# Bfloat16 constants loaded into place, first weights requested ahead of them, row statistics moved behind the queries: the opening of a four-layer attention kernel

## The chip, the cores and the metric

The kernel runs on one core of a Trainium2 chip. The metric is the device time of one execution in microseconds (us). Three runs of the kernel before the change took 3129.34, 3132.39 and 3118.13 us; their median is 3129.34.

Engines are named as in the profile: PE is the matrix engine, DVE the vector engine, ACT the scalar engine, POOL GpSimd. SP issues DMAs and computes nothing; POOL issues DMAs too. Each engine works through its own instructions strictly in the order in which they stand.

## The reference, cut to what matters

Two layers alternate twice on x, a float32 array of 2048 rows (tokens) by 512 columns.

```
x = x + A(layernorm(x));  x = x + B(layernorm(x));  and both once more
A: q = x@wq in 32 heads of 16; one shared k = x@wk and v = x@wv (16 wide)
   softmax(q k / 4) v for every head, then @ wo
B: 32 heads, 4 segments of 512 tokens; causal attention within a segment,
   joined by the gate sigmoid(beta) with a running memory of earlier segments, then @ wo
layernorm: (x - mean) / sqrt(var + 1e-5), no weights
```

## The kernel before

Tokens go in four blocks (b = 0 to 3) of 512, and a block in four tiles of 128 rows. Numbers that need more than bfloat16 are kept as a high and a low part (`xh`, `xl` for the normed and transposed input, `w[:, 0]` and `w[:, 1]` for a weight), so a projection of one block is 12 matmuls of 512 columns: high by high, high by low, low by high, for each of four slices of 128 input columns. All four tiles of a block must be in `xh` and `xl` before its projection can start.

The program is generated by coroutines. `prep()` makes layer A's keys for block after block: `norm_tiles` (normalise on DVE into `xn`, transpose on PE, copy to `xh`, subtract to `xl`), `a_keys` (project K, split it into float16 parts, write `kst` and `va`), and for block 0 `a_queries`. `norm_stats` computes mean and variance of a block's rows: BN_STATS and BN_AGGR for each tile, then some twelve tiny operations for the inverse root. While block b is at work, `prep()` loads the x tiles of block b+1 and issues their `norm_stats` ahead of time; the `xt` pool has four buffers, so each load waits until a tile of block b has been normalised.

Each of the four queries projections of block 0 takes its weight from `wload`: POOL requests the float32 weight into a `wst` buffer, POOL writes the high part, DVE subtracts to make the low part (line 306), and POOL stores both parts to memory for later use. There are two `wst` buffers. Before the change they also hold, one after another, the constant masks on the way to their bfloat16 copies, and `w0`, the K and V weight. Query parts are written to memory by SP (`sd`, line 656) and read back in the layout of the scores (`qa`, lines 699 and 700).

A score tile is eight small matmuls (`qa`, `kst`), two heads by 512 queries for 128 keys; ACT takes its exponential into `pa` (line 790); two score tiles are followed on PE by eight matmuls with `va`, which accumulate in the banks `pva`. When a unit (a pair of head groups over a range of keys) ends, DVE transposes `pva` away (lines 828 and 829), and only then can the next unit's products start. The first 64 score tiles of the kernel need the keys of block 0 alone: eight units of four key tiles. Then come units of twelve key tiles, whose first eight need blocks 1 and 2 and the last four block 3. So the 81st score tile is the first that needs block 3.

`weave` mixes the score coroutine with `prep()` by a planner's clock: every generator step says when, by fixed costs, it will be ready, and the one with the best estimate is recorded next. The recorded steps are then placed by the tile framework's scheduler. An edit of the beginning can therefore move instructions well beyond it.

Of the kernel before, what the change touches and what calls it, by code (L numbers as in the profile page):

```python
# [29 lines left out]
F32 = mybir.dt.float32  # L30
F32R = mybir.dt.float32r
BF16 = mybir.dt.bfloat16
# [6 lines left out]
P = 128  # L39
S, D, H, DH = 2048, 512, 32, 16  # L40
NB, BT = 4, 512
# [10 lines left out]
TA0 = 60e3  # L52
TA1 = 110e3

C_ID, C_BM, C_SEL, C_MQ, C_MK, C_BN, C_BK, C_MV = 0, 128, 136, 144, 656, 784, 912, 1040
S_X, S_H, S_L, S_G = 0, 4, 5, 6
C_MW = C_MV + 512
C_N = C_MW + 512
# [2 lines left out]
def shape_constants():  # L61
    import numpy as np

    c = np.zeros((P, C_N), np.float32)
    r = np.arange(P)
    c[:, C_ID:C_ID + P] = np.eye(P)
    c[:, C_MQ + 384:C_MQ + 512] = np.where(r[None, :] > r[:, None], NEG, 0.0)
    c[:, C_MK:C_MK + P] = np.where(r[None, :] < r[:, None], NEG, 0.0)
    for t in range(4):
        for h in range(8):  # L70
            c[16 * h:16 * h + 16, C_BN + 32 * t + 8 * t + h] = 0.515625
    c[0:16, C_BK:C_BK + P] = 0.515625
    for t in range(4):
        for i in range(2):
            at = 32 * t + np.arange(32)
            c[64 * i:64 * i + 32, C_MV + P * t:C_MV + P * t + P] = np.where(r[None, :] < at[:, None], NEG, 0.0)
            c[64 * i:64 * i + 32, C_MW + P * t:C_MW + P * t + P] = np.where(r[None, :] > at[:, None], NEG, 0.0)
    for h in range(8):
        c[16 * h:16 * h + 16, C_BM + h] = 1.0
    for g, part in enumerate((0, 1, 0, 2, 1, 0)):  # L80
        c[16 * g:16 * g + 16, C_SEL + part] = 1.0
    c[96:98, C_SEL + 3] = -1.0
    for i in range(2):
        c[64 * i:64 * i + 16, C_SEL + S_H] = 1.0
        c[64 * i + 16:64 * i + 32, C_SEL + S_L] = 1.0
        c[64 * i + 32:64 * i + 48, C_SEL + S_H] = 1.0
        c[64 * i + 48, C_SEL + S_G] = -GUARD_K
    return c


@with_exitstack
def net_kernel(ctx, tc, x_in, a_wq, a_wk, a_wv, a_wo, b_wq, b_wk, b_wv, b_wo, b_beta, cst, out):
# [76 lines left out]
    def st(shape, dt, tag):  # L169
        return one.tile(shape, dt, tag=tag, name=nm(tag))  # L170

    def tmp(n, shape, dt, tag):
        return pools[n].tile(shape, dt, tag=tag, name=nm(tag))

    def f(ap):
        return ap.bitcast(F32)
# [36 lines left out]
        return r  # L213

    x_0 = load_x(0)
    cs = st([P, C_MQ], F32, "cs")
    nc.sync.dma_start(cs, cst[:, 0:C_MQ])
    c1 = tmp(2, [P, 512], F32, "wst")
    nc.sync.dma_start(c1, cst[:, C_MQ:C_MK])
    c2 = tmp(2, [P, 512], F32, "wst")[:, 0:C_MV - C_MK]  # L220
    nc.sync.dma_start(c2, cst[:, C_MK:C_MV])
    ident = cs[:, C_ID:C_ID + P]
    maskq = st([P, 512], BF16, "maskq")
    V.tensor_copy(maskq, c1)
    bmask = cs[:, C_BM:C_BM + 8]
    sel = [cs[:, C_SEL + i:C_SEL + i + 1] for i in range(7)]
    idb = st([P, P], BF16, "idb")
    V.tensor_copy(idb, ident)
    maskk = st([P, P], BF16, "maskk")
    V.tensor_copy(maskk, c2[:, C_MK - C_MK:C_MK - C_MK + P])  # L230
    bnq = st([P, 4, 32], BF16, "bnq")
    V.tensor_copy(bnq.rearrange("p t h -> p (t h)"), c2[:, C_BN - C_MK:C_BN - C_MK + P])
    bnk = st([P, P], BF16, "bnk")
    V.tensor_copy(bnk, c2[:, C_BK - C_MK:C_BK - C_MK + P])
    maskv = st([P, 4, P], BF16, "maskv")
    maskw = st([P, 4, P], BF16, "maskw")
    for m_, at in ((maskv, C_MV), (maskw, C_MW)):
        c3 = tmp(2, [P, 512], F32, "wst")
        nc.sync.dma_start(c3, cst[:, at:at + 512])
        V.tensor_copy(m_.rearrange("p c k -> p (c k)"), c3)  # L240
    ones = st([P, 32], BF16, "ones")
    G.memset(ones, 1.0)
    wmx = st([32, 8], F32, "wmx")
# [86 lines left out]


    wkv_d = dram.tile([P, 2, 512], F32, tag="wkv_d", name="wkv_d")
    w0 = tmp(2, [P, 512], F32, "wst")
    for r in range(8):
        src = (a_wv if r == 7 else a_wk).rearrange("(k p) c -> p k c", p=P)
        nc.sync.dma_start(w0.rearrange("p (k r c) -> p k r c", k=4, r=8)[:, :, r, :], src,
                          allow_slow_non_contiguous=True)
    w1 = tmp(6, [P, 2, 512], F32R, "w")
    V.tensor_copy(w1[:, 0, :], w0)  # L339
    V.tensor_tensor(w1[:, 1, :], w0, f(w1[:, 0, :]), op=ALU.subtract)  # L340
    nc.sync.dma_start(wkv_d, f(w1))
    wq_["ready"].append(("Akv", 0, w1))


# [165 lines left out]
    def norm_stats(xt, tiles, t0):  # L510

        n = len(tiles)
        mv = tmp(2, [P, 4, 2], F32, "mv")
        for j in range(n):
            s6 = tmp(2, [P, 6], F32, "s6")
            V.bn_stats(s6, xt[tiles[j]])
            V.bn_aggr(mv[:, j, :], s6)
        ve = tmp(2, [P, 4], F32, "ve")[:, 0:n]
        V.tensor_scalar_add(ve, mv[:, 0:n, 1], 1e-5)
        sh = tmp(2, [P, 4], I32, "sh")[:, 0:n]  # L520
        V.tensor_scalar(sh, ve.bitcast(I32), 1, None, op0=ALU.logical_shift_right)
        yi = tmp(2, [P, 4], I32, "yi")[:, 0:n]
        V.tensor_scalar(yi, sh, -1, 0x5F3759DF, op0=ALU.mult, op1=ALU.add)
        y = yi.bitcast(F32)
        for _ in range(3):
            y2 = tmp(2, [P, 4], F32, "y2")[:, 0:n]
            V.scalar_tensor_tensor(y2, y, -0.5, y, op0=ALU.mult, op1=ALU.mult)
            V.tensor_tensor(y2, y2, ve, op=ALU.mult)
            yn = tmp(4, [P, 4], F32, "yn")[:, 0:n]
            V.scalar_tensor_tensor(yn, y2, 1.5, y, op0=ALU.add, op1=ALU.mult)  # L530
            y = yn
        return mv, y, on("dve", t0, n * 700 + 2300)
# [88 lines left out]
    def a_queries(L, b, aw, early=False, spare=False):  # L621

        sqs = []

        def guard(a, z, tq):

            h = 8 * (z - a)
            ps, rel = yield from slot(lambda s: s[0:h, :], tq, "cols")
            for t in range(a, z):
                T.matmul(ps, lhsT=bnq[:, t, 8 * a:8 * z], rhs=sqs[t], start=t == a, stop=t == z - 1)  # L630
            mr = tmp(1, [32, 512], F16, "mr")[0:h]
            V.tensor_scalar_mul(mr, ps, UP * UP / GUARD_K)
            c = b if h == 32 else NB + a
            V.reduce_max(L["qmx"][0:h, c:c + 1], ps, axis=AX.X)  # L634
            nc.sync.dma_start(L["sd"][b][8 * a:8 * z, 32, :], mr)
            t1 = on("dve", pe(220 * (z - a), "cols"), 1200)
            rel(t1)
            return t1 + LOAD

        for t in range(4):  # L640
            w = aw[1 + t] if aw is not None else wget("Aq", 1)[0]
            ps, e, rel = yield from project_t(w)
            qf, t1 = evac(ps, e)
            rel(t1)
            if not L["exact"]:
                sq = tmp(4, [P, 512], BF16, "sqq")
                if spare:
                    V.tensor_tensor(sq, qf, qf, op=ALU.mult)
                    tq = on("dve", t1, 602)
                else:  # L650
                    A.activation(sq, qf, AF.Square)
                    tq = on("act", t1, 478)
                sqs.append(sq)
            qp, t1 = (split3 if L["exact"] else split2)(qf, t1)
            for c in range(3 if L["exact"] else 2):
                nc.sync.dma_start(L["sd"][b][8 * t:8 * t + 8, 16 * c:16 * c + 16, :], qp[:, c, :])
            t2 = t1 + LOAD
            if early:
                t2 = max(t2, (yield from guard(t, t + 1, tq)))
                L["qr"][b][t] = t2  # L660
        if not early:
            if not L["exact"]:
                t2 = max(t2, (yield from guard(0, 4, tq)))
            L["qr"][b] = [t2] * 4
# [556 lines left out]
    def everything(exact):  # L1221
# [21 lines left out]
        def prep():  # L1243
            for b in range(NB):
                if exact:
                    xt, st_ = load_x(b), None
                elif b == 0:
                    xt, st_ = x_0, None
                else:
                    xt, st_ = ahead.pop(b)  # L1250
                for tiles in ((0, 1), (2, 3)) if st_ is None else ((0, 1, 2, 3),):
                    yield from norm_tiles(xt, tiles, clk["pe"] + LOAD, st_)
                if b < NB - 1 and not exact:
                    xt = load_x(b + 1)
                    ahead[b + 1] = xt, norm_stats(xt, (0, 1, 2, 3), clk["pe"] + LOAD)
                yield from a_keys(L, b, aw)
                if b == 0 or exact:
                    yield from a_queries(L, b, aw, not exact)
                evac_on[0] = "dve"

        def late():
# [115 lines left out]
```

## Time and profile before

| | |
|---|---|
| runs | 3129.34, 3132.39, 3118.13 us |
| profiled execution | 3124.81 us, span 3123.0 us |
| granted PE clock, mean | 0.976 |
| PE busy | 2776.1 us (89%) |
| ACT busy | 2323.0 us (74%) |
| DVE busy | 1581.4 us (51%) |
| first score matmul / first query projection / K projection of block 0 start | 46.28 / 26.97 / 21.03 us |

The span runs from the first to the last instruction; the execution's time is 1.81 us more. Busy shares are means over the kernel. In the list of groups a row reads: line, engine, operation, output<-input with shapes, count, then busy time, mean length of one, and the idle time just before them with what ended it. In the timeline a row is start, length, engine, line, operation; a bracket gives the idle time before it and what ended it.

### The profile page before, as it was taken

How to read it: one execution, taken by the hardware profiler on the slowest of the kernel's cores; microseconds unless marked ns; L12 is line 12 of the kernel's file. 1: busy time of each engine (PE TensorE's matmuls, PEld its weight loads, DVE VectorE, ACT ScalarE, POOL GpSimd, SP SyncE). 2: the span in 40 equal slices, each digit the busy share in tenths (PEclk: the TensorE clock that was granted, in tenths of full speed). 3: DMA queues.
4: the chain of work that ended last, by engine and by line, in shares of the span. 5: the costliest groups of instructions: out<-in, count | busy, mean ns of one | idle time of the engine just before them, and what ended most of it. 6: DMA issues, size and time to landing. Idle time of an engine off the chain costs nothing.

```text
span 3123.0 us, 115586 instructions
## 1 busy us (share of the span) xinstructions
PE 2776.1 (89%) x51746; PEld 1324.5 (42%) x51746; DVE 1581.4 (51%) x4515; ACT 2323.0 (74%) x2519; POOL 278.4 (9%) x437
## 2 busy tenths in 40 slices
PE   6899888999898998889998898988998899898977
PEld 3444443445443453344544344434443445343543
DVE  6644345534555435564455545456345643555465
ACT  4788777886788767787688878668688887888433
POOL 2001120001000010000100010000000001000111
PEclk9999999999999999999999999999999999999978
DMA  5212231113311233112422142311331113211331
GB/s 156 79 53 81 91 121 47 40 61 108 102 40 42 68 106 95 39 43 71 136 78 73 38 137 96 122 48 51 115 97 45 42 30 127 66 42 46 127 106 38
DMA packets 153596, 242.30 MB, mean 78 GB/s; under 512 B 26272, under 2 KB 101888, under 8 KB 153088
## 3 DMA queue, kind: packets, MB, share of 16 engines
q1 hardware_dynamic: 124672, 132.03, 14.2%
q0 software_dynamic: 28416, 102.77, 10.3%
q8 instruction: 407, 6.67, 0.9%
q14 instruction: 101, 0.83, 0.1%
HBM read 164.21 MB, written 70.52 MB: 75 GB/s over the span
## 4 chain that ended last, share of the span: by engine, by line
PE 38%; ACT 24%; issue 18%; DVE 10%; DMA 6%; POOL 2%; SPq 1%; DVEq 0%; ACTq 0%; POOLq 0%
ACT pa L790 20%; PE bank L101 18%; PE bank L481 13%; PE bank L104 7%; ACT pa L1066 3%; DVE mo L1030 3%; DMA sb<-parts 3%; DMA xt<-in_A_x_dram 1%; DVE parts L579 1%; DMA qkb<-sb 1%; POOL parts L577 1%; DMA wst<-in_B_wk_dram 0%; PE bank L541 0%; DVE qf L559 0%; DVE m L1001 0%
## 5 line engine op out<-in xcount | busy, mean ns | idle before, releaser
L790 ACT ACTIVATE pa<-bank 128x1024 f32<-128x1024 f32 x2048 | 1952.1, 1041 | 458.2 <-PE bank L104 451.9
L104 PE MATMUL bank<-pa,va 64*17 64x512 f32 x14336 | 1101.9, 598 | 0.0
L101 PE MATMUL bank<-pa,va 64*17 64x512 f32 x2048 | 1057.7, 597 | 8.6 <-DVE ts L828 8.0
L101 PE MATMUL bank<-qa,kst 49*32 49x512 f16 x2048 | 741.5, 381 | 159.2 <-ACT pa L790 108.2
L104 PE MATMUL bank<-qa,kst 49*32 49x512 f16 x14336 | 816.8, 386 | 1.9 <-DVE qmx L634 1.9
L1030 DVE CUSTOM_DVE_ANT_0 mo<-bank,maskq 128x256 bf16<-128x256 f32 (+3 forms) x896 | 438.6, 490 | 297.6 <-PE bank L104 239.8
L104 PEld LDWEIGHTS <-kst 49*32 49x32 f16 x14336 | 224.3, 90 | 502.5 <-issue 490.9
L101 PE MATMUL bank<-qkb 48*32 48x384 f16 (+6 forms) x1472 | 331.3, 305 | 94.7 <-DVE m L1030 33.7
L1066 ACT ACTIVATE pa<-bank 128x1024 f32<-128x1024 f32 x320 | 317.4, 1033 | 82.9 <-PE bank L104 79.7
L104 PE MATMUL bank<-qkb 48*32 48x512 f16 (+7 forms) x6720 | 354.1, 311 | 12.4 <-DVE m L1001 10.8
L101 PEld LDWEIGHTS <-kst 49*32 49x32 f16 x2048 | 172.3, 91 | 382.6 <-issue 354.3
L481 PE MATMUL bank<-xh,w 128*128 128x512 f32 x832 | 296.9, 416 | 9.7 <-DVE w L339 4.5
L104 PEld LDWEIGHTS bank<-pa,va 64*17 64x17 f32 x14336 | 256.7, 94 | 26.1 <-DVE t L829 12.1
L481 PE MATMUL bank<-w,xh 128*128 128x512 f32 x752 | 244.6, 407 | 3.7 <-issue 2.0
L101 PEld LDWEIGHTS bank<-pa,va 64*17 64x17 f32 x2048 | 187.7, 94 | 105.4 <-issue 16.7
L104 PEld LDWEIGHTS <-qkb 50*32 50x32 f16 (+1 forms) x6720 | 151.1, 93 | 186.2 <-issue 177.7
L293 POOL DMA_DIRECT2D w<-wd x154 | 85.4, 554 | 1390.8 <-PE bank L481 1207.9
L481 PEld LDWEIGHTS bank<-xh,w 128*128 128x128 f32 x832 | 158.9, 191 | 85.3 <-issue 41.8
L101 PEld LDWEIGHTS <-qkb 48*32 48x32 f16 (+1 forms) x1472 | 123.5, 93 | 130.2 <-issue 86.3
L559 DVE COPY qf<-bank 128x512 f32<-128x512 f32 x91 | 62.8, 690 | 213.9 <-PE bank L481 213.9
L104 PE MATMUL bank<-pa,vb 128*17 128x384 f32 (+3 forms) x1920 | 165.3, 447 | 4.0 <-ACT pa L1066 3.6
L481 PE MATMUL bank<-xl,w 128*128 128x512 f32 x416 | 167.6, 403 | 0.2 <-DVE xl L549 0.2
(171 smaller groups left out, 2679.3 us busy)
## 6 DMA issues: line engine op xcount, KB each, us to landing
w<-wd POOLq DMA_DIRECT2D x154, 512.0 KB, 5.0
sb<-parts SPq DMA_DIRECT2D x192, 128.0 KB
qkb<-sb SPq DMA_DIRECT2D x256, 96.0 KB
wd<-w POOLq DMA_DIRECT2D x24, 512.0 KB, 4.0
x<-xt SPq DMA_DIRECT2D x48, 256.0 KB
xt<-x SPq DMA_DIRECT2D x48, 256.0 KB
qa<-sd SPq DMA_DIRECT2D x176, 66.0 KB
xt<-in_A_x_dram SPq DMA_DIRECT2D x40, 256.0 KB
```

Of the source, the lines that this page charges most:

```text
L101: nc.tensor.matmul(*a, **k)
L104: tc.keep_in_program_order(nc.tensor.matmul(*a, **k))
L293: G.dma_start(f(w), parts_d[kind, i])
L481: T.matmul(ps, lhsT=l_(kt), rhs=r_(kt), start=n == 0, stop=n == 11)
L559: V.tensor_copy(x, ps)
L577: G.tensor_scalar(parts[:, 0, :], x, up, 0.0, op0=ALU.mult, op1=ALU.add)
L579: V.scalar_tensor_tensor(parts[:, 1, :], x, up, parts[:, 0, :], op0=ALU.mult, op1=ALU.subtract)
L790: A.activation(x, sc, AF.Exp, scale=scale)
L1030: V.tensor_tensor_reduce(out=mo[:, 0:nk], in0=ps[:, o_:o_ + nk], in1=maskq[:, 512 - nk:512], op0=ALU.add, op1=ALU.max, scale=1.0, scalar=- ...
L1066: A.activation(e, sc, AF.Exp, scale=0.25 if exact else 0.25 / (UPB * UPB))
```

## The change

Four things, all in the opening of the program.

1. The masks and small matrices are stored in the constant array as bfloat16 pairs (rounded on the host) and are loaded straight into two tiles, `halves` (128x256 and 128x768 words, read as bfloat16). Seven DVE casts (`maskq`, `idb`, `maskk`, `bnq`, `bnk`, `maskv`, `maskw`) and the loads through `wst` are gone.
2. `w0` is requested right after the small constants and ahead of the larger masks and of the eight loads of the gate (`gv`); the same rows are fetched by four loads of 128x7x16 and one of 128x4x16 in place of eight of 128x4x16.
3. The store of the split K weight (`wkv_d`) is issued in `prep()` after the x tiles of block 1.
4. `norm_stats` of block b+1 is issued after `a_keys` (and `a_queries`) of block b; the load of its tiles stays where it was.

```diff
-C_ID, C_BM, C_SEL, C_MQ, C_MK, C_BN, C_BK, C_MV = 0, 128, 136, 144, 656, 784, 912, 1040
+C_ID, C_BM, C_SEL, C_HALF = 0, 128, 136, 144
+C_IB, C_MK, C_BN, C_BK, C_MQ, C_MV = 144, 272, 400, 528, 656, 1168
...
-    return c
+    c[:, C_IB:C_IB + P] = np.eye(P)
+    u = np.ascontiguousarray(c[:, C_HALF:]).view(np.uint32)
+    u = ((u + 0x7fff + ((u >> 16) & 1)) >> 16).astype(np.uint16)
+    return np.concatenate([c[:, 0:C_HALF], u.view(np.float32)], axis=1)
...
-    cs = st([P, C_MQ], F32, "cs")
-    nc.sync.dma_start(cs, cst[:, 0:C_MQ])
-    c1 = tmp(2, [P, 512], F32, "wst")
-    nc.sync.dma_start(c1, cst[:, C_MQ:C_MK])
-    c2 = tmp(2, [P, 512], F32, "wst")[:, 0:C_MV - C_MK]
-    nc.sync.dma_start(c2, cst[:, C_MK:C_MV])
+    cs = st([P, C_HALF], F32, "cs")
+    nc.sync.dma_start(cs, cst[:, 0:C_HALF])
+    halves = []
+    for a, z in ((C_IB, C_MQ), (C_MQ, C_N)):
+        h_ = st([P, (z - a) // 2], F32, f"halves{a}")
+        halves.append((h_, C_HALF + (a - C_HALF) // 2))
+    nc.sync.dma_start(halves[0][0], cst[:, halves[0][1]:halves[1][1]])
+    w0 = tmp(2, [P, 512], F32, "wst")
+    w0_ = w0.rearrange("p (k r c) -> p k r c", k=4, r=8)
+    for k in range(4):
+        src = bass.AP(tensor=a_wk.tensor, offset=a_wk.offset + k * P * DH, ap=[[DH, P], [0, 7], [1, DH]])
+        nc.sync.dma_start(w0_[:, k, 0:7, :], src, allow_slow_non_contiguous=True)
+    nc.sync.dma_start(w0_[:, :, 7, :], a_wv.rearrange("(k p) c -> p k c", p=P), allow_slow_non_contiguous=True)
+    nc.sync.dma_start(halves[1][0], cst[:, halves[1][1]:halves[1][1] + (C_N - C_MQ) // 2])
+    small, masks = (x.bitcast(BF16) for x, _ in halves)
...
-    maskq = st([P, 512], BF16, "maskq")
-    V.tensor_copy(maskq, c1)
...
-        c3 = tmp(2, [P, 512], F32, "wst")
-        nc.sync.dma_start(c3, cst[:, at:at + 512])
-        V.tensor_copy(m_.rearrange("p c k -> p (c k)"), c3)
+    idb, maskk = small[:, 0:P], small[:, P:2 * P]
+    maskq = masks[:, 0:512]
...
     wkv_d = dram.tile([P, 2, 512], F32, tag="wkv_d", name="wkv_d")
-    w0 = tmp(2, [P, 512], F32, "wst")
-    for r in range(8):
-        src = (a_wv if r == 7 else a_wk).rearrange("(k p) c -> p k c", p=P)
-        nc.sync.dma_start(w0.rearrange("p (k r c) -> p k r c", k=4, r=8)[:, :, r, :], src,
-                          allow_slow_non_contiguous=True)
...
-    nc.sync.dma_start(wkv_d, f(w1))
...
                 if b < NB - 1 and not exact:
                     xt = load_x(b + 1)
-                    ahead[b + 1] = xt, norm_stats(xt, (0, 1, 2, 3), clk["pe"] + LOAD)
+                    t_ = clk["pe"] + LOAD
+                    if b == 0:
+                        nc.sync.dma_start(wkv_d, w1.bitcast(F32))
                 yield from a_keys(L, b, aw)
                 if b == 0 or exact:
                     yield from a_queries(L, b, aw, not exact)
+                if b < NB - 1 and not exact:
+                    ahead[b + 1] = xt, norm_stats(xt, (0, 1, 2, 3), t_)
```

What stands in the built program, at three places. `order` rows are line, operation, output<-inputs; a number behind a name only tells buffers apart; lines of the kernel after the change are four lower from the middle of the file on.

SP's queue after the x tiles of block 0, before the change:

```order
L217 DMA cs_89<-in_cst_dram 128x144
L219 DMA wst_91<-in_cst_dram 128x512
L221 DMA wst_93<-in_cst_dram 128x384
L349 DMA gv_174<-in_B_beta_dram 128x1x1 x4
L239 DMA wst_107<-in_cst_dram 128x512
L239 DMA wst_110<-in_cst_dram 128x512
L349 DMA gv_174<-in_B_beta_dram 128x1x1 x3
L336 DMA wst_161<-in_A_wk_dram 128x4x16 x7
L336 DMA wst_161<-in_A_wv_dram 128x4x16
```

The same place now:

```order
L221 DMA cs_89<-in_cst_dram 128x144
L226 DMA halves_6_91<-in_cst_dram 128x256
L231 DMA wst_94<-in_A_wk_dram 128x7x16 x4
L232 DMA wst_94<-in_A_wv_dram 128x4x16
L233 DMA halves_7_92<-in_cst_dram 128x768
L345 DMA gv_152<-in_B_beta_dram 128x1x1 x8
```

The K weight has moved ahead of the masks and the gate, and nothing in front of it waits for a `wst` buffer.

DVE after the block's K projection (`va` and `kmx` read its result; `w_205` and `w_212` are the low parts of the first two query weights, `parts` the low part of K), before:

```order
L306 TENSOR_TENSOR w_205<-wst_203,w_205 128x512
L517 BN_AGGR mv_327<-s_115_334 128x2
L516 BN_STATS s_116_337<-xt_325 128x6
L517 BN_AGGR mv_327<-s_116_337 128x2
L519 TENSOR_SCALAR ve_340<-mv_327 128x4
L521 TENSOR_SCALAR sh_342<-ve_340 128x4
L523 TENSOR_SCALAR yi_344<-sh_342 128x4
L306 TENSOR_TENSOR w_212<-wst_210,w_212 128x512
```

And now (`w_183` and `w_190` are the same two weights):

```order
L512 BN_STATS s_156_676<-xt_303 128x6
L607 COPY va_15_111<-bank 128x4x16
L513 BN_AGGR mv_666<-s_156_676 128x2
L515 TENSOR_SCALAR ve_679<-mv_666 128x4
L614 TENSOR_REDUCE kmx_180<-bank 128x1
L308 TENSOR_TENSOR w_183<-wst_181,w_183 128x512
L308 TENSOR_TENSOR w_190<-wst_188,w_190 128x512
```

The last statistics of block 1 and the reduction of K now stand ahead of both weights, which follow one another; before, the first weight stood ahead of the last statistics.

PE ahead of the K projection of block 3 (`w_170`; its first matmul is the row L481), before:

```order
L101 MATMUL bank<-pa_1918,va_23_123 17x512
L104 MATMUL bank<-pa_1918,va_23_123 17x512 x3
L104 MATMUL bank<-pa_1902,va_23_123 17x512 x4
L481 MATMUL bank<-xh_156,w_170 128x512
L481 MATMUL bank<-xl_157,w_170 128x512
L481 MATMUL bank<-xh_156,w_170 128x512 x2
```

And now (`w_149` is the K weight, `xn_...` the normed tiles of block 3; the row of the first tile, `xn_1745`, stands one score tile further up):

```order
L108 MATMUL bank<-pa_1885,va_15_111 17x512 x4
L537 MATMUL bank<-cs_89,xn_1893 128x128 x4
L537 MATMUL bank<-cs_89,xn_1927 128x128 x4
L537 MATMUL bank<-cs_89,xn_1935 128x128 x4
L477 MATMUL bank<-xh_144,w_149 128x512
L477 MATMUL bank<-xl_145,w_149 128x512
```

Before, the four transposes of block 3 (four matmuls each) stand behind the 65th, 68th, 73rd and 77th score tile and are thus spread among scores; now they stand behind the 79th and, three in a row, the 80th. The K projections of blocks 1, 2 and 3 stood behind the 33rd (half of it behind the 36th), the 59th and the 80th score tile; now they stand behind the 40th, the 67th and the 80th. From a little behind the keys of block 3 on, every engine has the same order in both kernels.

More of the change, by code (lines that the diff above doesn't have):

```diff
@@ L222, in net_kernel @@
+    small, masks = (x.bitcast(BF16) for x, _ in halves)
     ident = cs[:, C_ID:C_ID + P]
-    maskq = st([P, 512], BF16, "maskq")
-    V.tensor_copy(maskq, c1)
     bmask = cs[:, C_BM:C_BM + 8]
     sel = [cs[:, C_SEL + i:C_SEL + i + 1] for i in range(7)]
[L227 to L237, printed above, removed]
-        c3 = tmp(2, [P, 512], F32, "wst")
-        nc.sync.dma_start(c3, cst[:, at:at + 512])
-        V.tensor_copy(m_.rearrange("p c k -> p (c k)"), c3)
+    idb, maskk = small[:, 0:P], small[:, P:2 * P]
+    bnq, bnk = small[:, 2 * P:3 * P].rearrange("p (t h) -> p t h", t=4), small[:, 3 * P:4 * P]
@@ L241, in net_kernel @@
+    maskq = masks[:, 0:512]
+    maskv = masks[:, 512:1024].rearrange("p (c k) -> p c k", c=4)
+    maskw = masks[:, 1024:1536].rearrange("p (c k) -> p c k", c=4)
     ones = st([P, 32], BF16, "ones")
```

## The prediction

> **What bounds the kernel now.** I read the page's head, the table by windows, then waits and timeline of the opening, since the change touches nothing later. From the page: span, the chain of work that ended last, and the largest group.
>
> ```profile
> span 3123.0 us, 115586 instructions
> PE 38%; ACT 24%; issue 18%; DVE 10%; DMA 6%; POOL 2%; SPq 1%; DVEq 0%; ACTq 0%; POOLq 0%
> L790 ACT ACTIVATE pa<-bank 128x1024 f32<-128x1024 f32 x2048 | 1952.1, 1041 | 458.2 <-PE bank L104 451.9
> ```
>
> PE and ACT pass score tiles to each other for the whole span (ACT takes 1041 ns for a tile's exponential). The order after the opening is the same in both kernels, so the question is at what time the opening hands over. By windows (start:end, length, then busy time of PE, PEld, DVE, ACT, POOL, granted PE clock, DMA share, GB/s):
>
> ```profile
> 60.00:80.00 20.00, 16.93 (x305) 6.49 (x312) 10.26 (x27) 15.23 (x17) 0.00 (x0) 1.00 0.22 68
> 160.00:200.00 40.00, 37.84 (x670) 15.84 (x676) 19.31 (x37) 35.73 (x40) 3.16 (x3) 1.00 0.18 49
> ```
>
> At 160 to 200 PE is busy for 37.84 of 40 us and ACT for 35.73: full. Time won or lost before that is kept, as no slack follows that could take it up. In the opening itself waits decide. The longest of the first 60 us (engine, line, waited for: total, times, longest):
>
> ```profile
> POOL wst L299 <- DVE maskw L240: 5.8, 1, 5.8
> DVE w L339 <- DMA wst<-in_A_wv_dram: 2.6, 1, 2.6
> PE bank L481 <- DVE w L339: 4.5, 1, 4.5
> SPq L239 <- DVE y L528: 3.5, 1, 3.5
> ```
>
> Here is the wait that the change aims at: SP holds mask loads until a `wst` buffer is cast away, the K weight stands behind them, DVE and PE wait for it. The timeline of that path up to the fifth exponential:
>
> ```profile
> 9.87 0.42 DVE L224 CAST maskq<-wst 128x512 bf16<-128x512 f32 x1
> 14.07 3.71 SPq L336 DMA_DIRECT2D wst<-in_A_wk_dram  x7
> 15.21 2.67 DVE L549 TENSOR_TENSOR xl<-bank,xh 128x512 fp32r<-128x512 f32 x4
> 20.45 0.43 DVE L339 CAST w<-wst 128x512 fp32r<-128x512 f32 x1 [2.58 <-DMA wst<-in_A_wv_dram]
> 20.92 0.69 DVE L340 TENSOR_TENSOR w<-wst,w 128x512 fp32r<-128x512 f32 x1
> 21.03 0.77 PE L481 MATMUL bank<-xh,w 128*128 128x512 f32 x1 [4.50 <-DVE w L339]
> 26.24 0.59 ACT L557 COPY qf<-bank 128x512 f32<-128x512 f32 x1 [2.81 <-PE bank L481]
> 28.90 0.69 DVE L516 BATCH_NORM_STATS2 s<-xt 128x6 f32<-128x512 f32 x1 [1.90 <-DMA xt<-in_A_x_dram]
> 36.61 0.67 DVE L579 SCALAR_TENSOR_TENSOR parts<-qf,parts 128x512 f16<-128x512 f32 x1
> 46.28 0.61 PE L101 MATMUL bank<-qa,kst 49*32 49x512 f16 x1 [2.29 <-DMA qa<-sd]
> 52.56 7.44 ACT L790 ACTIVATE pa<-bank 128x1024 f32<-128x1024 f32 x8 [1.05 <-PE bank L104]
> ```
>
> And the stretch from there to the first score of block 3's keys, the 81st tile, at 147.83. Three DVE copies of `qf` are the K projections of blocks 1, 2 and 3:
>
> ```profile
> 77.80 1.03 PE L101 MATMUL bank<-pa,va 64*17 64x512 f32 x2 [0.93 <-DVE ts L828]
> 88.40 0.69 DVE L559 COPY qf<-bank 128x512 f32<-128x512 f32 x1 [0.26 <-PE bank L481]
> 97.32 1.03 PE L101 MATMUL bank<-pa,va 64*17 64x512 f32 x2 [1.29 <-DVE ts L828]
> 112.92 0.50 PE L481 MATMUL bank<-xh,w 128*128 128x512 f32 x1
> 116.10 0.69 DVE L559 COPY qf<-bank 128x512 f32<-128x512 f32 x1 [1.43 <-PE bank L481]
> 125.18 0.54 DVE L538 TENSOR_SCALAR xn<-xt,mv,yn 128x512 f32<-128x512 f32 x1
> 128.54 0.69 DVE L516 BATCH_NORM_STATS2 s<-xt 128x6 f32<-128x512 f32 x1 [0.99 <-DMA xt<-in_A_x_dram]
> 129.49 0.68 DVE L547 CAST xh<-bank 128x512 fp32r<-128x512 f32 x1
> 130.54 0.68 DVE L549 TENSOR_TENSOR xl<-bank,xh 128x512 fp32r<-128x512 f32 x1
> 137.16 0.66 PE L541 MATMUL bank<-cs,xn 128*128 128x128 f32 x4
> 139.40 0.37 PE L101 MATMUL bank<-qa,kst 49*32 49x512 f16 x1 [0.17 <-ACT pa L790]
> 140.60 0.50 PE L481 MATMUL bank<-xh,w 128*128 128x512 f32 x1
> 143.26 0.40 PE L481 MATMUL bank<-xh,w 128*128 128x512 f32 x1
> 143.77 0.69 DVE L559 COPY qf<-bank 128x512 f32<-128x512 f32 x1 [4.50 <-PE bank L481]
> 147.83 0.39 PE L101 MATMUL bank<-qa,kst 49*32 49x512 f16 x1
> ```
>
> Between 139.40 (the 80th tile's scores) and 147.83 stands a gap of 8.4 us: block 3's keys are late already.
>
> **The start, a gain.** Seven casts leave DVE, the largest 0.42; all stood ahead of the last `xl`, but the split of the K weight (0.43 + 0.69) now stands there instead. I let the two cancel but for 0.3 us, so `xl` ends at 17.6 in place of 15.21 + 2.67 = 17.9. The weight's requests no longer wait on SP: they start at about 3.5 in place of 14.07. From first request to cast it was 20.45 - 14.07 = 6.4; the same rows behind the x tiles come by 10 to 12, and DVE reaches the cast at about 12.4. So the K projection waits for `xl` alone: 17.65 in place of 21.03, a gain of 3.4. Bounds: no gain where DVE must stand for the weight until 16; 3.7 where the casts' removal counts in full. The first query weight needs no buffer either (the 5.8 on POOL go), but its low part now stands on DVE behind the reduction of K, so POOL's gain is not passed on.
>
> From the copy of K to the low part of the first query it was 37.28 - 26.24 = 11.0, with 1.90 of DVE standing for an x tile. That tile now comes earlier, but a second weight's difference (of L340's length, 0.69) and the statistics' tiny operations stand in the path. Bounds 9.1 and 11.7; I take 10.5. With 5.2 for the projection (21.03 to 26.24) the part is ready at 17.65 + 5.2 + 10.5 = 33.4, 3.9 earlier. Its way through memory stays as it was: first score at 42.4. The store of the K weight is the only one moved behind the x tiles; nobody reads it for hundreds of microseconds, so I cost it at nothing. Gate loads come later, but their exponential on ACT needs them only before the copy of K at 22.9, several microseconds behind their issue. Half of the last query's projection, its copy and its square now stand behind the first scores, 1.1 us on ACT: fifth exponential at 52.56 - 3.9 + 1.1 = 49.8, a gain of 2.8.
>
> **Blocks 1 to 3, a loss.** The pace is the trace's: from the fifth exponential (52.56) to block 2's projection behind the 59th tile (112.92) are 60.4 us; less a projection of block 1 (140.60 to 143.6, 3.0) and two waits for DVE (0.93, 1.29) that is 55.1 for 54 tiles, 1.02 each. Now that projection stands behind the 67th tile: 49.8 + 62 x 1.02 + 3.0 + 2.2 = 118.2, and ends at 121.2, where before it ended at about 116. Block 3's first transpose stands behind the 79th tile: 12 x 1.02 and 0.7 for transposes of K later, 134.1. What then follows runs on DVE and PE with nothing to cover it, as two of the others stand behind the 80th tile and each link waits for the one before:
> - `xh` 0.68 and `xn` 0.54;
> - the load of an x tile for the later queries into the buffer just freed (125.18 + 0.46 to 128.54: 2.9) and its statistics, 0.69 and a short second step that I put at 0.2, ahead of the rest on DVE;
> - two `xh`, two `xl` at 0.65 in line, 2.6;
> - the last `xn` 0.54, its transpose 0.66, `xh` and `xl` 0.68 each.
>
> That is 10.2: projection at 144.3, copied at 147.5. From copy to the 81st tile it was 147.83 - 143.77 = 4.06: the 81st tile at 151.6, 3.7 later than before, though the start is 2.8 to 3.9 earlier. The delayed statistics themselves cost nothing: DVE issues them behind work that is more urgent, with waits for x tiles that it has before too.
>
> In the sum I add half of a further cost. After the pause of 4.50 at 21.03 the matmuls of 512 columns ran at 0.43 each and came to 0.235 only after 4.4 us of work:
>
> ```profile
> 22.02 1.05 PE L481 MATMUL bank<-xh,w 128*128 128x512 f32 x2
> 22.87 0.63 PE L481 MATMUL bank<-xl,w 128*128 128x512 f32 x1
> 29.44 0.63 PE L481 MATMUL bank<-xh,w 128*128 128x512 f32 x2
> 29.91 0.40 PE L481 MATMUL bank<-xl,w 128*128 128x512 f32 x1
> ```
>
> (starts 22.02 to 22.87 for two, 29.44 to 29.91 for two). If PE, nearly idle from 134 to 144, slows down as it did there, block 3's projection takes 12 x 0.2 = 2.4 longer. Half of it gives +3.7 + 1.2 = +4.9. The Trainium skill, "TensorE: Matmul & The Clock Gate", Part 1, says that the matrix clock is halved after a window of about 3.4 us without work and comes back after as long a busy one; by that rule the slow projection is certain here and the sum would be +6.1. The trace agrees in size (4.4 us at half pace after 4.5 us of pause), though a chain with four short bursts of transposes in it is shown by no row.
>
> **Sum.** The profiled execution took 3124.81 (span 3123.0 and 1.8 around it), 4.5 below the median. It becomes 3129.7, the median 3129.34 + 4.9 = 3134.2. Less than 0.5% (15.6 us) can hardly be told from no change by runs that lie between 3118 and 3132.
>
> **Rivals.**
> - *The start's gain is kept* (faster): the gap before the 81st tile stays at 8.4, because block 3's transposes are ready as soon as PE reaches them and the x tile comes early. For it speaks that DVE is busy only for 10.26 of 20 us at 60 to 80; against it the order, in which one `xh` on DVE cannot precede a transpose that PE does behind the 79th tile. It gives -2.8: 3126.5.
> - *Start and loss cancel*: the K projection of block 0 runs at 0.235 because the pause before it shrinks from 4.5 to about 1 us, 2.4 more at the start and for all that follows, with block 3's at full pace. 3.7 - 2.4 = +1.3: 3130.6.
> - *Slower by over 0.5%*: DVE stands at the K weight's cast, in line ahead of the last two `xn`, because 4096 short rows now compete with the x tiles. It decides from an arrival after 16 on; each microsecond later delays everything. With arrival at 19 the start loses 3.0 where it gained 3.4, and with the slow projection of block 3 the sum is 3.7 + 6.4 + 2.4 = +12.5: 3141.8, a little short of the mark, which 3 us of chance then pass.
>
> **How the numbers follow.** The forecast (+2.5 to +8) 0.55, gain kept 0.20, cancelled 0.17, the late weight 0.08. Runs scatter by 5 us to either side of a median. The likeliest alone reaches from 3128 to 3141; with the scatter and the two cases below it I give 3120 to 3144, which leaves out the upper part of the last case and the lowest of the second. Slower by over 0.5%: most of the last case and the tail of the first, 0.08. Faster by over 0.5%: 0.02, for no case gives it without scatter.
>
> **What would show it.** In the profile after: the first K projection near 17.7 and the first score near 42.4 (right start); the K weight's cast with no wait for a DMA; the copy of block 2's K near 121.5 (before 116.10); three transposes in a row near 135 to 143 with ACT idle; the 81st tile near 151.6 to 154. Wrong would be a first score not earlier than 45 (rival four), or a gap before the 81st tile of 9 us or less (rival one). If windows after 160 are emptier than before, time is given back and my claim that nothing follows to take it up is wrong.

## The result and the profile after

Six runs of the changed kernel took 3140.03 to 3144.83 us, median 3143.01; the kernel before, beside them, 3117.43 to 3132.39, median 3122.82. The ratio is 1.0055, 95% interval [1.0039, 1.0070]: 12 to 22 us slower. The forecast of 3134.2 (+4.9) had the direction but was far short in size: the medians differ by 20.2 us. A second series of seven runs gave 1.0043 [1.0025, 1.0061]. The profiled execution after took 3141.73 us, span 3139.9, clock 0.974.

The page of the profile after: its head and its largest group.

```profile
span 3139.9 us, 115569 instructions
L786 ACT ACTIVATE pa<-bank 128x1024 f32<-128x1024 f32 x2048 | 1951.5, 1041 | 461.3 <-PE bank L108 454.5
```

The exponential still takes 1041 ns, and its wait for PE grew only from 451.9 to 454.5 us over the span. So the tiles are no slower; the difference must lie ahead of them and in single pauses. The timeline of the opening after (start, duration, engine, line; behind the text, in brackets, the idle time before and what ended it):

```profile
8.52 6.85 SPq L345 DMA_DIRECT2D gv<-in_B_beta_dram  x8
12.75 0.43 DVE L336 CAST w<-wst 128x512 fp32r<-128x512 f32 x1
15.49 5.26 SPq L215 DMA_DIRECT2D xt<-in_A_x_dram  x4
17.53 0.79 PE L477 MATMUL bank<-xh,w 128*128 128x512 f32 x1 [0.68 <-ACT xh L540]
23.94 0.21 ACT L347 ACTIVATE gv<-gv 128x8 f32<-128x8 f32 x1 [6.46 <-DMA xt<-in_A_x_dram]
24.05 0.57 ACT L553 COPY qf<-bank 128x512 f32<-128x512 f32 x1
24.18 0.17 DVE L348 TENSOR_SCALAR gv<-gv 128x8 f32<-128x8 f32 x1 [5.98 <-ACT gv L347]
28.82 1.28 DVE L308 TENSOR_TENSOR w<-wst,w 128x512 fp32r<-128x512 f32 x2
29.55 1.22 PE L477 MATMUL bank<-xh,w 128*128 128x512 f32 x2 [1.97 <-DVE w L308]
36.98 0.67 DVE L575 SCALAR_TENSOR_TENSOR parts<-qf,parts 128x512 f16<-128x512 f32 x1
46.81 0.60 PE L105 MATMUL bank<-qa,kst 49*32 49x512 f16 x2
53.54 4.66 ACT L786 ACTIVATE pa<-bank 128x1024 f32<-128x1024 f32 x5
```

The K weight is there in time: its cast at 12.75 waits for no DMA, and the K projection begins at 17.53 (before 21.03). Then eight gate loads have taken SP for 6.85 us in one piece, the next block's x tiles stand behind them, and ACT and DVE stand for the gate until 23.94 and 24.18. (The row at 23.94 names an x tile as what ended ACT's wait, but the instruction reads `gv` alone; in kernel 1 below, the same row has a wait of 5.65 us and names the gate's loads.) DVE's weight differences come at 28.82 and the low part of the first query at 36.98, where it was 36.61: the 3.5 us won are gone. The first score is at 46.81 (before 46.28).

The stretch up to the 81st tile, after:

```profile
136.91 0.66 PE L537 MATMUL bank<-cs,xn 128*128 128x128 f32 x4
145.11 0.94 PE L537 MATMUL bank<-cs,xn 128*128 128x128 f32 x4 [3.84 <-DVE xn L534]
146.84 0.80 PE L477 MATMUL bank<-xh,w 128*128 128x512 f32 x1 [0.78 <-DVE xh L543]
148.16 1.05 PE L477 MATMUL bank<-xh,w 128*128 128x512 f32 x2
149.01 0.63 PE L477 MATMUL bank<-xl,w 128*128 128x512 f32 x1
152.58 0.69 DVE L555 COPY qf<-bank 128x512 f32<-128x512 f32 x1 [2.33 <-PE bank L477]
153.31 0.63 ACT L590 ACTIVATE sqq<-qf 128x512 bf16<-128x512 f32 x1 [14.20 <-DVE qf L555]
157.37 0.61 PE L105 MATMUL bank<-qa,kst 49*32 49x512 f16 x1
162.65 0.69 DVE L555 COPY qf<-bank 128x512 f32<-128x512 f32 x1 [5.19 <-PE bank L477]
```

ACT stands for 14.20 us ahead of the square of block 3's keys. The same row in the kernel before:

```profile
144.49 0.63 ACT L594 ACTIVATE sqq<-qf 128x512 bf16<-128x512 f32 x1 [3.25 <-DVE qf L559]
```

There it is 3.25 us. Block 3's projection starts two matmuls of 512 columns every 0.85 us (148.16 to 149.01), half the speed of the 0.47 seen at 29.44 in the kernel before. Copied at 152.58 where it was 143.77, it lets the 81st tile start at 157.37 (before 147.83), and the next projection is copied at 162.65 (before 152.41): +10.2 us. From here on both kernels have the same instructions in the same order on every engine.

### The profile page after: what moved, and what is told of

Its sections match the earlier page's. It is cut to its first block, busy times and chain, and to the rows that moved or that the text cites. A ratio compares the mean times of both kernels' runs of the same rounds, so it can differ in the third digit from the quotient of the medians.

```text
span 3139.9 us, 115569 instructions
## 1 busy us (share of the span) xinstructions
PE 2781.5 (89%) x51746; PEld 1330.4 (42%) x51746; DVE 1579.6 (50%) x4508; ACT 2322.0 (74%) x2519; POOL 279.7 (9%) x437
## 3 DMA queue, kind: packets, MB, share of 16 engines
q0 software_dynamic: 28416, 102.77, 10.2%
## 4 chain that ended last, share of the span: by engine, by line
PE 38%; ACT 23%; issue 20%; DVE 10%; DMA 5%; POOL 2%; SPq 1%; DVEq 0%; ACTq 0%; POOLq 0%
ACT pa L786 19%; PE bank L105 17%; PE bank L477 13%; PE bank L108 7%; DVE mo L1026 3%; ACT pa L1062 3%; DMA sb<-parts 3%; DMA xt<-in_A_x_dram 1%; DMA qkb<-sb 1%; DVE parts L575 1%; PE bank L537 1%; POOL parts L573 1%; DVE m L997 0%; DVE qf L555 0%; DMA w<-wd 0%
## 5 line engine op out<-in xcount | busy, mean ns | idle before, releaser
L786 ACT ACTIVATE pa<-bank 128x1024 f32<-128x1024 f32 x2048 | 1951.5, 1041 | 461.3 <-PE bank L108 454.5
L1026 DVE CUSTOM_DVE_ANT_0 mo<-bank,halves 128x256 bf16<-128x256 f32 (+3 forms) x896 | 438.6, 489 | 301.4 <-PE bank L108 244.8
```

Source lines behind the costliest of these rows:

```text
L786: A.activation(x, sc, AF.Exp, scale=scale)
L1026: V.tensor_tensor_reduce(out=mo[:, 0:nk], in0=ps[:, o_:o_ + nk], in1=maskq[:, 512 - nk:512], op0=ALU.add, op1=ALU.max, scale=1.0, scalar=- ...
```

## Experiments

Each kernel is timed beside the kernel before on the same chip. As a second measure I take from its trace the start of the 193rd exponential, at 265 to 280 us, behind the whole opening. Kernels 11 and 12 are the kernel before again; with the first trace it stands there at 268.5, 266.2 and 268.0, mean 267.6, and offsets are against that. Every offset is read from one trace, and these three of one kernel already lie 2.3 us apart.

**Kernel 1: statistics back.** In the changed kernel:

```diff
-                    t_ = clk["pe"] + LOAD
+                    ahead[b + 1] = xt, norm_stats(xt, (0, 1, 2, 3), clk["pe"] + LOAD)
...
-                if b < NB - 1 and not exact:
-                    ahead[b + 1] = xt, norm_stats(xt, (0, 1, 2, 3), t_)
```

> The changed kernel with one part undone: the next block's statistics stand again ahead of the keys' projection; masks, weights and gates as changed. On PE the projections and transposes of blocks 1 to 3 then stand behind the same score tiles as in the kernel before. Theory A (the loss comes from the statistics' new place, by way of the gap ahead of the 81st tile): first score near 46.8 as after, 81st tile at 148 to 150, time 0 to 4 us above the kernel before. Theory B (the loss comes from the gate loads in line ahead of ACT and DVE at 24 us): 81st tile 155 or later, time 14 to 20 us above before.

**Kernel 2: only the statistics later**, in the kernel before:

```diff
-                    ahead[b + 1] = xt, norm_stats(xt, (0, 1, 2, 3), clk["pe"] + LOAD)
+                    t_ = clk["pe"] + LOAD
...
+                if b < NB - 1 and not exact:
+                    ahead[b + 1] = xt, norm_stats(xt, (0, 1, 2, 3), t_)
```

> The kernel before with one part of the change alone: the statistics later. Masks, weights, gates as before. Theory A: first score near 46.3, 81st tile at 156 to 158, time 10 to 18 us above before. Theory B: 81st tile within 2 us of 147.8, time within 4 us of before.

**Kernel 3: gates later**, in the changed kernel:

```diff
+    def gates():
+        for p in range(2):
+            for t in range(4):
...
         while L["qr"][0][0] > 1e17:
             clk["pe"] = max(clk["pe"], next(zb)())
+        gates()
```

> The changed kernel with the eight gate loads and their arithmetic written behind the first block's queries. Both theories: copy of the first K near 23.1 and first score at 41 to 43. Theory A: the four transposes of block 3 still stand behind tiles 79 and 80, so most of the loss stays: 81st tile at 152 to 154, time 9 to 14 us above before. Theory B: 81st tile at 147 or earlier, time at before's or up to 5 us below it.

**Kernel 4: both, gates later and statistics back.**

> The changed kernel with both: gates behind the first block's queries, statistics back ahead of the keys. Theory A with the gates as a second, smaller loss: first score at 41 to 43, 81st tile at 143 to 146, time 2 to 5 us below before. If time won at the start is taken up again later (a theory C, against my claim that nothing follows to take it up): 81st tile early, but time within 1 us of before.

| kernel | statistics | gates | 5th exponential | late queries' first copy | offset at 193rd exponential | ratio of times, 95% interval |
|---|---|---|---|---|---|---|
| changed | late | in line | 53.54 | 162.65 | +11.5 | 1.0055 [1.0039, 1.0070] |
| 1 | early | in line | 51.45 | 153.50 | +2.3 | 1.0018 [1.0007, 1.0028] |
| 2 (old masks) | late | as before | 52.25 | 159.71 | +8.1 | 1.0057 [1.0038, 1.0076] |
| 3 | late | later | 46.73 | 157.17 | +5.8 | 1.0023 [1.0012, 1.0034] |
| 4 | early | later | 50.07 | 149.12 | -2.1 | 1.0004 [0.9992, 1.0016] |

The same row of the timeline, ACT's wait for block 3's keys, in kernels 1, 2, 3 and 4:

```profile
147.13 0.63 ACT L590 ACTIVATE sqq<-qf 128x512 bf16<-128x512 f32 x1 [3.32 <-DVE qf L555]
```
```profile
151.81 0.63 ACT L594 ACTIVATE sqq<-qf 128x512 bf16<-128x512 f32 x1 [14.06 <-DVE qf L559]
```
```profile
149.27 0.63 ACT L592 ACTIVATE sqq<-qf 128x512 bf16<-128x512 f32 x1 [14.28 <-DVE qf L557]
```
```profile
142.75 0.63 ACT L592 ACTIVATE sqq<-qf 128x512 bf16<-128x512 f32 x1 [3.26 <-DVE qf L557]
```

Late statistics: 14 us; early ones: 3.3, whatever the masks and gates do. Theory A, that the loss comes from the statistics' new place, is shown from both sides (kernel 1 takes it away, kernel 2 alone makes it): 9.2 us between the changed kernel and kernel 1, 7.9 between kernels 3 and 4, 8.1 for kernel 2 against before. In time kernel 2 fell into theory A's 10 to 18 us; kernel 1 came 2 to 9 us above before, where A had 0 to 4 and B 14 to 20. The 81st tile started at 150.5 in kernel 1 and 155.5 in kernel 2, each half a microsecond outside theory A's range and far from B's. The gates of theory B are the second part: 5.7 between the changed kernel and kernel 3, 4.4 between kernels 1 and 4. The gate rows of kernel 3 show why:

```profile
11.07 0.82 SPq L215 DMA_DIRECT2D xt<-in_A_x_dram  x2
14.11 1.22 SPq L215 DMA_DIRECT2D xt<-in_A_x_dram  x2
15.38 6.44 SPq L349 DMA_DIRECT2D gv<-in_B_beta_dram  x7
22.81 0.59 ACT L555 COPY qf<-bank 128x512 f32<-128x512 f32 x1 [6.08 <-PE bank L479]
24.38 1.28 DVE L308 TENSOR_TENSOR w<-wst,w 128x512 fp32r<-128x512 f32 x2
27.37 0.21 ACT L350 ACTIVATE gv<-gv 128x8 f32<-128x8 f32 x1 [3.31 <-DMA gv<-in_B_beta_dram]
```

The x tiles go first, the copy of K is at 22.81 and the differences at 24.38 in place of 28.82; the gate's exponential at 27.37 keeps nobody from the next query. Kernel 3 moves the loads and the arithmetic on them together, so how much belongs to SP's line and how much to DVE's is not shown. Kernel 3's time, 4 to 11 us above before, lies between the two theories (9 to 14, and 0 or less), as it must where both causes are real. The first score came at 39.07, earlier than the 41 to 43 expected, and the first exponential starts at 41.91 (after: 48.72). What remains of the change, with the gates later (kernel 4: bfloat16 masks, early weights, the moved store), has an offset of -2.1 us, which is no more than traces of one kernel differ by; in time, too, it can't be told from nothing. That kernel's expected 2 to 5 us below before were not reached, its 81st tile came at 146.1, not 143 to 146, and its first score at 45.3, not 41 to 43: with the statistics early, DVE does them ahead of the query weights (the second pair of weights at 35.70, in kernel 3 at 33.39).

**Kernel 5: the changed kernel again.**

> The changed kernel as it is, to see how much of its loss is the same in every execution. Half-clock time is taken as 2 x (1 - granted clock) x span of each run; over the four earlier kernels a microsecond of it goes with 0.37 us of time. If the loss beyond the 10.2 us of the opening is chance of half-clock stretches: first score 46.8, 81st tile within 1 us of 157.4 and the late queries' copies 10 us behind before again, but a total between 3128 and 3145 that follows the half-clock time. If a cost after the opening is fixed: total 3139 to 3146 with half-clock time no longer than before's 142.

The late copy stands at 163.46 and the offset is +12.0: the opening repeats. The median was 3132.18 (3126.38 to 3138.52). The rest, from the 193rd exponential to the end, took 2860.8 us in the first trace of this kernel and 2850.8 in this one, and 2854.5, 2846.1 and 2852.3 in the three traces of the kernel before. By span and clock of the execution before and after, and of kernels 5, 11 and 12:

```profile
core 0: 3123.0 us, clock 0.976
```
```profile
core 0: 3139.9 us, clock 0.974
```
```profile
core 0: 3130.4 us, clock 0.977
```
```profile
core 0: 3112.4 us, clock 0.978
```
```profile
core 0: 3120.3 us, clock 0.976
```

The trace's clock records suggest why equal work differs by 10 us: the PE clock is granted at half for stretches of mostly 3.41, 6.83 or 10.24 us, once 27.3 us near the end. In the first trace of the changed kernel 20 of 28 such stretches come within 6.8 us of a pause of PE of over 1 us. Over the 160 timed runs of kernels 1 to 10 and of the kernel before beside them, compared within each kernel, a microsecond of half clock (2 x (1 - clock) x span, known to about 3 us) goes with 0.41 us of time, correlation 0.82. By that the two traces of the changed kernel, with 163 and 144 us of half clock, should lie 8 us apart. A correlation doesn't show which is the cause: longer pauses would lengthen both. So the expectation "chance of half-clock stretches" fits what lies behind the opening, without being shown; but the changed kernel also has more of them, 151 us on average against 138 beside it, and by its first trace four stretches, 23.9 us, in the opening, where the first trace of the kernel before has three, 13.7.

**Kernel 6: PE kept busy.** Ahead of each of block 3's transposes in the changed kernel:

```diff
+            if busy[0]:
+                for k in range(10):
+                    T.matmul(ps.rearrange("p k c -> p (k c)"), lhsT=idb, rhs=maskq, start=True, stop=True)
```

> The changed kernel with ten matmuls of 512 columns, whose result is not used, ahead of each of block 3's four transposes, so that PE has work while it waits there. Theory H (block 3's K projection ran at half pace because PE stood idle ahead of it): its matmuls at 0.235 in place of 0.43, its copy 2 to 3 us earlier than 152.6, time 2 to 5 us below the changed kernel. Rival: pace and copy as in the changed kernel or up to 2 us later, since the added matmuls only stand ahead of the transposes.

```profile
141.44 2.33 PE L540 MATMUL bank<-halves,halves 128*128 128x512 bf16 x10
150.33 0.50 PE L477 MATMUL bank<-xh,w 128*128 128x512 f32 x1 [0.93 <-DVE xh L548]
151.39 0.63 PE L477 MATMUL bank<-xh,w 128*128 128x512 f32 x2
151.86 0.40 PE L477 MATMUL bank<-xl,w 128*128 128x512 f32 x1
153.99 0.69 DVE L560 COPY qf<-bank 128x512 f32<-128x512 f32 x1 [1.54 <-PE bank L477]
161.07 0.69 DVE L560 COPY qf<-bank 128x512 f32<-128x512 f32 x1 [2.51 <-PE bank L477]
```

The clock from 147 to 161 us, in the changed kernel and in kernel 6 (the last three numbers: granted clock, DMA share, GB/s):

```profile
147.00:161.00 14.00, 11.74 (x45) 7.32 (x46) 7.04 (x23) 2.57 (x3) 2.85 (x4) 0.62 0.31 100
```
```profile
147.00:161.00 14.00, 10.62 (x70) 6.29 (x75) 9.07 (x26) 2.57 (x3) 2.81 (x4) 1.00 0.30 104
```

With PE busy the clock is 1.00 and two matmuls start every 0.47 us: from its first matmul to the copy the projection takes 3.66 us, in the changed kernel 5.74; the next takes 7.08 from copy to copy in place of 10.07. So a PE with too little to do made them slow, worth 2.1 and 3.0 us. (The Trainium skill, "TensorE: Matmul & The Clock Gate", Part 1, has a rule of this kind, half clock after an idle window of some 3.4 us.) The pause of 3.84 us ahead of the transposes at 145.11 agrees with it. The second slow stretch came without such a pause: in the 3.4 us ahead of it PE worked for 1.33 us, and its longest pause was 1.41 us. In the changed kernel:

```profile
152.20:155.60 3.40, 1.33 (x9) 0.59 (x8) 2.51 (x6) 0.63 (x1) 2.73 (x4) 1.00 0.00 0
155.60:162.40 6.80, 6.61 (x28) 3.79 (x28) 1.83 (x8) 1.94 (x2) 0.12 (x1) 0.50 0.47 158
```

Theory H was right about the pace and wrong about what it would win. The added matmuls gave it back: they stand ahead of the transposes, the projection starts at 150.33 in place of 146.84, its copy comes 1.4 us later than in the changed kernel, as the rival had it, and the time did not fall (ratio 1.0055 [1.0037, 1.0073]).

**Kernels 7 and 8: the pause itself.** One number in the changed kernel (7) and in kernel 3 (8):

```diff
-TA0 = 60e3
+TA0 = 42e3
```

> The changed kernel with one number changed: the planner's estimate for the first 128 tiles is 42 in place of 60 us, which sets blocks 1 to 3 among earlier tiles; block 3's transposes then stand behind tiles 68, 71, 74 and 76 and its projection behind the 78th. First score as in the changed kernel. Theory A (the pause ahead of the 81st tile is the loss of blocks 1 to 3): the pause of 20 us on ACT shrinks to under 8 us, time 8 to 16 us below the changed kernel. Rival: the projections' time only moves ahead of other tiles, time within 4 us of the changed kernel.

> The changed kernel with the gate loads behind the first block's queries and the planner's estimate at 42. Both repairs: first score at 41 to 43, pause ahead of the 81st tile under 8 us, late queries' first copy at 138 to 146 (before 152.4), time 6 to 14 us below the kernel before. If the pauses only move: 0 to 5 us above before, as with the gates alone.

Both missed. From the start of one exponential to the next, the longest pause on ACT shrank from 20.0 us (138.04 to 158.07, ahead of the 81st tile) to 9.3 in kernel 7 (140.80 to 150.06, ahead of the 79th, since the projection now stands behind the 78th), and the late queries' first copy came at 157.29; but another pause grew later:

```profile
150.06 1.02 ACT L786 ACTIVATE pa<-bank 128x1024 f32<-128x1024 f32 x1 [8.23 <-PE bank L108]
207.34 0.69 DVE L512 BATCH_NORM_STATS2 s<-xt 128x6 f32<-128x512 f32 x1 [3.15 <-DMA xt<-in_A_x_dram]
212.62 0.50 PE L477 MATMUL bank<-xh,w 128*128 128x512 f32 x1 [2.21 <-DVE xh L543]
216.05 1.94 ACT L786 ACTIVATE pa<-bank 128x1024 f32<-128x1024 f32 x2 [4.37 <-PE bank L108]
```

The late queries' statistics now wait for an x tile, PE for DVE, ACT for PE. By the 193rd exponential the offsets are +11.1 (changed: +11.5) and +5.6 (kernel 3: +5.8). Ratios: 1.0064 [1.0045, 1.0082] and 1.0044 [1.0028, 1.0060]. Kernel 8's late copy came at 151.51, not 138 to 146, and its time is 9 to 19 us above before, more than even the rival's 0 to 5; why it should be slower than kernel 3 at the same offset stays open. By the offsets, the pause of 14 us marks where the late statistics are paid for; moving the projections to earlier tiles moves the bill and doesn't lower it.

**Kernels 9 and 10: kernel 4 with `TA0` at 50 and 42.**

> The fourth kernel (gates behind the first block's queries, statistics ahead of the keys) with the planner's estimate at 50 in place of 60: the keys' projections of blocks 1 to 3 stand behind tiles 28, 51 and 71 (before 33, 59 and 80). If the pause ahead of the 81st tile (8.1 us on ACT in the kernel before) can be taken away so: pause under 4 us, late queries' fourth copy 8 to 12 us earlier than before's 152.4, time 5 to 11 us below before. Rival, from the seventh kernel: the pause comes back at the late queries (200 to 220 us), time within 3 us of before or above it.

> The same with the estimate at 42: projections behind tiles 28, 49 and 70, and the late queries' transposes from tile 74 on. Expected by the two readings as for 50; if pauses only move, this one loses more, 3 to 8 us above before, since the late queries' loads and transposes crowd at 200 to 220 us as in the seventh kernel.

Kernel 9: median 3119.74 against 3119.54, ratio 1.0005 [0.9991, 1.0019]; no pause is left ahead of its 81st tile (the nearest, 4.6 us from 139.52 to 144.10, is ahead of the 78th, while PE projects the late queries), its late copy is 9.8 us ahead of before's 152.4, but its offset at the 193rd exponential is -1.0. Kernel 10: 1.0019 [1.0006, 1.0031], offset +7.6. The rival's reading held for both; no version beat the kernel before.

**Kernels 11 and 12: the kernel before again.**

> The kernel before as it is, for a second profile. The offsets of all kernels were read against one profiled execution of it; four of them have totals 2.5 to 7.5 us worse than their opening says. If that execution's opening was slow by chance: the late queries' first copy at 147 to 151 here. If openings repeat: within 1 us of 152.4, and then the rest is lost after 160 us.

> The same, for a third profile; expected as the run ahead of it.

The block-3 copy and the late queries' first copy, kernel 11, then 12:

```profile
143.06 0.69 DVE L559 COPY qf<-bank 128x512 f32<-128x512 f32 x1 [4.50 <-PE bank L481]
150.15 0.69 DVE L559 COPY qf<-bank 128x512 f32<-128x512 f32 x1 [2.52 <-PE bank L481]
```
```profile
144.91 0.69 DVE L559 COPY qf<-bank 128x512 f32<-128x512 f32 x1 [4.50 <-PE bank L481]
152.01 0.69 DVE L559 COPY qf<-bank 128x512 f32<-128x512 f32 x1 [2.53 <-PE bank L481]
```

One opening is 2.3 us earlier than the first profile's, the other 0.4: neither expectation fits both. One trace carries about 2 us of chance by 152 us, and 8 us more by the end.

## Why the prediction was right in direction and short in size

The range of 3120 to 3144 was wide for the scatter of the runs, and the median of 3143.01 lies 1 us inside its upper end: that it holds is partly luck. The likeliest case, +2.5 to +8, was too small, and a loss of over 0.5%, which the first series shows (the second has 0.43%), had a chance of 0.08, mostly by a late K weight that did not happen.

- *First K projection at 17.65, weight's cast without a wait*: measured 17.53 and no wait. Right; the late weight (rival four) did not happen, though its sign of a first score after 45 did, by another cause.
- *"Gate loads come later, but their exponential on ACT needs them only before the copy of K at 22.9"*: the step that failed. It looked at ACT alone. The loads take 6.85 us of SP's line ahead of the x tiles, the gate's exponential came at 23.94 and not before 22.9, and the gate's arithmetic stands in DVE's line ahead of the statistics and the weight differences. The fifth exponential came at 53.54, forecast 49.8: 3.7 us short. Kernel 3, without that line, has it at 46.73, even ahead of the forecast. The order on DVE and SP showed both lines beforehand.
- *Blocks 1 to 3*: from the fifth exponential to the copy of block 3's keys the forecast had 147.5 - 49.8 = 97.7, with half of the slow projection 98.9. Measured 152.58 - 53.54 = 99.0. The chain from the first of block 3's transposes to the projection was forecast at 10.2; 146.84 - 136.91 = 9.9. The chain is right; that the whole agrees to 0.1 us is luck, since the way to the projection took 93.3 us (forecast 94.5) and the projection itself up to its copy 5.74 (forecast 3.2, with half of the slow pace 4.4).
- *"The delayed statistics themselves cost nothing"*: what they take on DVE no run separates, but their place moved everything of blocks 1 to 3, and kernels 1 and 2 put 8 to 9 us on it. The prediction had the chain just named as a loss of 3.7 us net of the start; it did not count the slow projections behind it in full.
- *Half of 2.4 us for a half-clock projection*: kernel 6 gives 2.1 for it, so all of it should have been counted, and the next projection ran slow too (10.07 from copy to copy, 7.09 to 8.64 in the kernel before): 1.4 to 3.0 us for which the sum had no term. The rule of the Trainium skill ("TensorE: Matmul & The Clock Gate", Part 1), quoted with "certain here", was the better guide for the first of the two; for the second it names no cause, as no pause there was as long. The row on which I had rested the half pace, block 0's projection behind a pause of 4.50 us, doesn't show the effect of that pause: in the changed kernel the same projection ran as slowly (18.84 to 19.70 for two) behind one of 0.68.
- *Sum*: +4.9 forecast; the miss of 3.7 at the start and 1.4 at the late projection make it 10.0, and the trace has 162.65 - 152.41 = 10.2 there (11.1 against the mean of the three traces of the kernel before).
- *"Time won or lost before 160 is kept"*: the loss is. From the 193rd exponential to the end one trace of the changed kernel lies among those of the kernel before and one 6 us above them (2850.8 and 2860.8 after; 2846.1 to 2854.5 before). By the traces, the opening accounts for about 12 of the 13 to 19 us between the means of the two series. Whether the few microseconds that are left are more than chance of the half clock stays open: two traces of one kernel differ by as much. Small gains of the opening (kernels 4 and 9) could not be found in the times.
- *Rivals*: "gain kept" and "start and loss cancel" needed a pause that stayed at 8 us or a projection of block 0 at full pace. The pause grew, and that projection's matmuls ran at 0.43 (17.53 to 22.6). Of the other signs, the copy of block 2's K came at 125.99, forecast 121.5: the late start, carried on.

## What to carry to other kernels

When small loads are moved, read what stands behind each of them on the issuing queue, and what stands behind the arithmetic on them on every engine: a gate that could come 3.4 us later at no cost (27.37 in kernel 3) kept DVE standing for 6 us because of its place in line. A planner that mixes two streams by estimates turns a harmless move at the start into a new order much later; look up where the last piece that the next unit needs has come to stand, and what then runs uncovered. And count a dependent chain with nothing beside it twice: once for its length, once for the slower matmuls that may stand behind it.

## What the hardware showed that was not expected

- The half clock comes in stretches of 3.41 us and multiples (3.41, 6.83, 10.24, once 27.3 in the trace), some 140 us of it per execution, and its run-to-run variation (118 to 170 us over the timed runs) goes along with most of the scatter of times: 0.41 us per us, correlation 0.82.
- Ten dummy matmuls of 512 columns (2.33 us) ahead of each of four transposes held the clock at 1.00 from 147 to 161 us, where it was 0.62 without them. Without them it was not always a pause of 3.4 us that halved the clock: at 155.6 it fell behind 3.4 us in which PE had worked for 1.33.
- The last of eight loads of the gate (128 values of four bytes each) was issued by 15.4 us, and the exponential that needs them started only at 23.94. In kernel 1 the trace names the loads themselves as what it waited for. The DMA view counts 715 packets of under 512 bytes between 11 and 18 us, and in kernel 3, where the gate comes later, 845 between 20 and 27 us, when hardly anything else moves (25 GB/s): 100 to 120 a microsecond. If each of the 1024 values is a packet of its own, eight loads take 9 to 10 us at that pace (an estimate), however few the bytes.
